# One DMA moved within SP's queue: a read back of turned attention weights, before or behind the next step's writes

## The chip, the cores and the metric

The kernel runs on one core of a Trainium2 chip. The metric is the device time of one execution in microseconds. Five engines take part: TensorE (PE) multiplies, VectorE (DVE), ScalarE (ACT) and GpSimd (POOL) do the work between, and SyncE (SP) issues the DMAs. Each engine runs its own instructions in the order in which the program lists them, and semaphores hold an instruction until what it needs is there.

## What is computed

A thresholded attention over 8 sequences, 8 heads, 576 tokens and head size 64, and behind it an expert layer with ELU.

```python
scores = scale * np.matmul(q, k.transpose(0, 1, 3, 2))
thresh = np.max(scores, axis=-1, keepdims=True) - tau
scores = np.where(scores >= thresh, scores, -1000000000.0)
attn = np.exp(scores - np.max(scores, axis=-1, keepdims=True))
attn = attn / (np.sum(attn, axis=-1, keepdims=True) + 1e-09)
attn_out = np.matmul(attn, v)
x = attn_out.transpose(0, 2, 1, 3).reshape(B * S, H * D)   # 4608 x 512
h = x @ w_in                                               # 512 x 2048
g = np.where(h > 0.0, h, np.exp(np.minimum(h, 0.0)) - 1.0)
out = g @ w_out                                            # 2048 x 512
```

All is in float32.

## The kernel before

**Pairs and steps.** The 64 heads are handled in 32 pairs of two heads. One step (a pair `pr` and a block `i`) takes 128 of the 576 query rows of both heads; blocks 0 to 3 are full, block 4 (`NC`) holds the last 64 rows of each head. Steps have numbers `n`. From number 20 on the five steps of a pair follow one another, so pair 7 is steps 35 to 39, and pair 8 is steps 40 to 44.

**One step.** TensorE makes the scores, VectorE the maxima, ScalarE the exponentials, VectorE and ScalarE mask them, and a normalization follows on POOL, VectorE or ScalarE (of step 41's two heads one is on ScalarE and one on POOL). Then the weights must be turned, so that TensorE can multiply them with the values. There are two ways. In one TensorE transposes 128x128 blocks. In the other (`turn_squares`, L859) VectorE transposes all 32x32 squares of the step into a tile `x` (L868, two buffers), SP writes it to a DRAM tile `there` in four DMAs of 144 KB, one for each quarter of the partitions (L893), and later `fetch` (L897) reads the step back in one DMA of 576 KB with the squares in their new places (L901; L910 for block 4). Blocks 0 and 1 of a pair are read into the tile `wTa`, blocks 2, 3 and 4 into `wTb`. Each of the two exists once. All steps around the change use the second way.

**Values.** `values(pr, 0)` (L915) multiplies `wTa` with the values of the pair, and so needs the reads of both block 0 and block 1: two matmuls at L925 and 16 at L930. A copy by ScalarE (L1060) puts the result into `xt`, the expert layer's input.

**Stages.** Steps 0 to 44 are the early stage. It shares TensorE with the plain expert layer of the first sequences (L1154). After step 44 the joined stage begins: the attention of the remaining pairs at L977, L1037, L1042 and L1050, and between them the expert layer of the earlier sequences, done with Strassen's seven products (L1678, L1818), whose sums of weights are read from DRAM as the tiles `sw` (L1250) and `t` (L1280). The end, from L2149 on, is the expert layer of the last two groups.

**What sets the order.** In the early stage every piece of work is a task with a due time, in the planner's own units. `task` (L1295) adds to a formula's due time an offset from the table `MOVED` under the task's name, such as `landed_40`. At the end (L1603) the tasks are issued in order of due time; `do` (L1299) first issues whatever a task names as needed. So a due time decides only the order in which instructions are listed, and with that the order on each engine and on SP's queue. Of a turned step, the task `turned` issues the transposes and the four writes, and the task `landed` issues the read back:

```python
if n < MIDDLE - 1:
    task(("turned", n), begin[n + 1] + 2.2, f"turn{k}", lambda pr=pr, i=i: turn_squares(pr, i), *norms)
if n < MIDDLE - 2:
    task(("landed", n), begin[n + 2] + 0.1, f"fetch{k}", lambda pr=pr, i=i: fetch(pr, i), ("turned", n), before)
```

Around the change the tasks that put a DMA on SP's queue come in this order (due times in brackets): `turned` 40 (1183), `landed` 39 (1188), `turned` 41 (1219), `landed` 40 (1222), `landed` 41 (1224), the output of pair 6, part 1 with a store to `xtail` (1225), `turned` 42 (1249), and then the loads of pair 9's values and of pair 10's keys. Between `turned` 41 and `landed` 40 stands an exponential of step 42 (1220), which is ScalarE's. `turned` 41 calls a normalization of step 41 on POOL that is needed and has not been issued by then. `values(8, 0)` comes much later in the list.

Of the kernel before, what the change touches and what calls it, by code (L numbers as in the profile page):

```python
# [131 lines left out]
    "landed_24": 486.39, "landed_25": 533.25, "landed_26": 984.59, "landed_27": 608.7, "landed_28": 593.43,  # L132
    "landed_29": 1100.39, "landed_3": 57.59, "landed_30": 602.25, "landed_31": 590.28, "landed_32": 704.7,
    "landed_33": 1197.19, "landed_34": 1068.39, "landed_35": 752, "landed_36": 789.43, "landed_37": 901.99,
    "landed_38": 847.93, "landed_39": 916.22, "landed_4": 23.49, "landed_40": 938.28, "landed_41": 938.99,
    "landed_42": 1089.42, "landed_5": 21.59, "landed_6": 85.49, "landed_7": 1161.59, "landed_8": 45.49, "landed_9":
    110.99, "late": 855.2, "load_k_1": 583, "load_k_10": 969.2, "load_k_2": 479, "load_k_3": 255, "load_k_4": 846,
    "load_k_5": 267.2, "load_k_6": 405.2, "load_k_7": 475.2, "load_k_8": 687.2, "load_k_9": 850.2, "load_q_1": 117,
# [2203 lines left out]
```

## Time and profile before

| What | us |
|---|---|
| median of 3 runs | 1265.59 |
| the runs, lowest and highest | 1262.77, 1266.57 |
| the profiled execution's own time | 1262.22 |
| its span, first to last instruction | 1260.4 |
| TensorE busy | 1245.6 |
| VectorE busy | 1041.4 |
| GpSimd busy | 729.4 |
| ScalarE busy | 636.4 |

The span is shorter than the time of the same execution, as it counts from the first instruction to the last. SP's DMA instructions are not counted as busy; the timeline of the queue gives for each how long SP took to issue it, and the DMA view how long from the issue until the data had landed. An idle time stands in brackets behind the group that it precedes, with what ended it as far as the trace can tell; "issue" there means that the trace shows no releaser.

Of the 16 DMA engines' time over the span, SP's queue takes 71.8%, in 323264 packets with 243.65 MB. The granted clock of TensorE was 0.999 on average.

### The profile page before, as it was taken

The page shows a single profiled execution, that of the slowest core. Times are in us where ns is not written, and L with a number is a line of the kernel's source. Part 1 is how long each engine was busy: PE and PEld are TensorE (multiplying, and loading weights), DVE is VectorE, ACT ScalarE, POOL GpSimd, SP SyncE. Part 2 cuts the span into 40 slices and gives each one's busy share as a digit, 9 for nine tenths or more (in the row PEclk, how much of TensorE's full clock was granted, in tenths as well). Part 3 has the DMA queues.
Part 4 walks back from the last instruction along what each step waited for, and adds up shares of the span by engine and source line. Part 5 has one row for each costly group of instructions (what it writes and reads, how often), then busy time and mean ns, then how long its engine had stood idle before and what let it go on. Part 6 is the DMA issues. An engine that isn't in the chain of part 4 may idle for free.

```text
span 1260.4 us, 21128 instructions
## 1 busy us (share of the span) xinstructions
PE 1245.6 (99%) x6598; PEld 956.5 (76%) x6598; DVE 1041.4 (83%) x2199; ACT 636.4 (50%) x1331; POOL 729.4 (58%) x1061
## 2 busy tenths in 40 slices
PE   8999999999999999999999999999999999999998
PEld 6675576467788787888788788878788887788876
DVE  7888777788898988898889889897889886776785
ACT  7999776664453526253534435352525352565321
POOL 4778655687575848676576757574867555122000
PEclk9999999999999999999999999999999999999999
DMA  7457788997989998898989888999889875000001
GB/s 144 146 172 181 173 243 229 264 279 196 233 238 254 247 252 228 228 264 221 268 211 259 221 243 218 255 247 251 234 229 264 221 224 173 20 1 1 1 34 34
DMA packets 325551, 245.74 MB, mean 195 GB/s; under 512 B 209216, under 2 KB 289984, under 8 KB 325440
## 3 DMA queue, kind: packets, MB, share of 16 engines
q1 hardware_dynamic: 323264, 243.65, 71.8%
q8 instruction: 52, 0.85, 0.3%
q10 hardware_dynamic: 2176, 0.75, 0.2%
q14 instruction: 59, 0.48, 0.1%
HBM read 154.53 MB, written 89.78 MB: 194 GB/s over the span
## 4 chain that ended last, share of the span: by engine, by line
PE 90%; DVE 4%; POOL 2%; DMA 2%; issue 1%; ACT 1%; SPq 1%; DVEq 0%; ACTq 0%; POOLq 0%
PE f L1678 22%; PE f L1818 22%; PE sc L977 8%; PE sc L1050 7%; PE f L2268 6%; PE f L2193 4%; PE f L1102 4%; PE sc L673 3%; PE f L1154 3%; PE pv L930 2%; PE f L2206 2%; PE rt L792 2%; PE sc L1042 1%; PE sc L1037 1%; DVE x L868 1%
## 5 line engine op out<-in xcount | busy, mean ns | idle before, releaser
L984 DVE TENSOR_REDUCE mx<-sc 128x1 f32<-128x576 f32 x207 | 148.3, 750 | 29.2 <-PE sc L977 25.2
L726 POOL TENSOR_SCALAR w<-w,rs 128x576 f32<-128x576 f32 x144 | 116.3, 816 | 70.3 <-DVE rs L789 70.1
L1004 ACT ACTIVATE w<-sc,mx 128x576 f32<-128x576 f32 x113 | 81.5, 740 | 115.0 <-DVE mx L984 98.0
L868 DVE STREAM_TRANSPOSE x<-w 128x512 f32<-128x512 f32 (+1 forms) x153 | 108.9, 744 | 13.1 <-POOL w L726 11.3
L996 POOL TENSOR_SCALAR th<-mx,ntau 128x2 f32<-128x2 f32 (+1 forms) x114 | 34.0, 298 | 132.8 <-DVE mx L984 132.8
L977 PE MATMUL sc<-kT,qT 64*128 64x448 f32 (+4 forms) x736 | 102.7, 416 | 0.0
L977 PEld LDWEIGHTS sc<-kT,qT 64*128 64x128 f32 x736 | 81.0, 186 | 24.3 <-issue 16.2
L1011 DVE SCALAR_TENSOR_TENSOR w<-sc,th,w 128x576 f32<-128x576 f32 x113 | 88.2, 810 | 9.5 <-ACT w L1004 9.2
L1678 PE MATMUL f<-xt,sw 128*128 128x256 f32 x384 | 93.6, 386 | 0.7 <-ACT g L1740 0.5
L1678 PE MATMUL f<-xt,w_in 128*128 128x256 f32 x384 | 92.0, 382 | 0.5 <-ACT w L1692 0.5
L1818 PE MATMUL f<-w_out,s 128*128 128x256 f32 x384 | 92.0, 382 | 0.1
L1818 PE MATMUL f<-w_out,g 128*128 128x256 f32 x384 | 92.0, 382 | 0.0
L1818 PE MATMUL f<-t,s 128*128 128x256 f32 x384 | 90.8, 379 | 0.0
L1678 PE MATMUL f<-x,w_in 128*128 128x256 f32 x384 | 90.8, 379 | 0.0
L726 POOL TENSOR_SCALAR e<-e,rs 128x576 f32<-128x576 f32 x91 | 67.4, 744 | 35.2 <-DVE rs L789 33.8
L1678 PEld LDWEIGHTS f<-xt,sw 128*128 128x128 f32 x384 | 69.3, 189 | 17.3 <-issue 5.0
L1678 PEld LDWEIGHTS f<-xt,w_in 128*128 128x128 f32 x384 | 71.9, 190 | 12.8 <-ACT w L1692 3.2
L1818 PEld LDWEIGHTS f<-w_out,g 128*128 128x128 f32 x384 | 72.0, 190 | 12.5 <-issue 3.2
L1818 PEld LDWEIGHTS f<-w_out,s 128*128 128x128 f32 x384 | 71.9, 190 | 12.5 <-issue 2.5
L1818 PEld LDWEIGHTS f<-t,s 128*128 128x128 f32 x384 | 72.8, 190 | 10.3 <-POOL s L1765 0.4
L1678 PEld LDWEIGHTS f<-x,w_in 128*128 128x128 f32 x384 | 72.9, 190 | 10.1 <-ACT s L1692 0.3
L1765 POOL TENSOR_TENSOR s<-g 128x256 f32<-128x256 f32 x96 | 75.0, 786 | 7.9 <-DVE g L1728 7.4
(345 smaller groups left out, 3113.5 us busy)
## 6 DMA issues: line engine op xcount, KB each, us to landing
there<-x SPq DMA_DIRECT2D x444, 144.0 KB, 3.5
wTb<-there SPq DMA_DIRECT2D x58, 576.0 KB, 6.4
wTa<-there SPq DMA_DIRECT2D x53, 576.0 KB, 5.0
sw<-win_sums SPq DMA_DIRECT2D x46, 384.0 KB, 4.7
t<-wout_sums SPq DMA_DIRECT2D x33, 512.0 KB, 6.1
qm<-in_q_dram SPq DMA_DIRECT2D x124, 72.0 KB, 4.9
wst<-in_moe_w_in_dram SPq DMA_DIRECT2D x16, 512.0 KB, 4.2
vm<-in_v_dram SPq DMA_DIRECT2D x64, 128.0 KB, 3.8
```

Source lines behind the costliest of these rows:

```text
L726: nc.gpsimd.tensor_scalar(wv, wv, st["rs"][:, h : h + 1], 1.0, ALU.mult, ALU.mult)
L868: nc.vector.transpose(x[:, :, c0 : c0 + nc_], src.rearrange("p (c g n) -> p g c n", c=nc_, n=T))
L977: on_banks(nc.tensor.matmul(o, qT[r, i * P : (i + 1) * P], kT[r, k0 : k0 + n], start=True, stop=True, skip_group_check=True), o)
L984: on_banks(nc.vector.tensor_reduce(st["mx"][:, h : h + 1], st["sc", h], axis=AX.XY if i == NC else AX.X, op=ALU.max, negate=True), st["sc" ...
L1004: on_banks(nc.scalar.activation(st["e", h], st["sc", h], AF.Exp, bias=st["mx"][:, h : h + 1]), st["sc", h])
L1011: on_banks(nc.vector.scalar_tensor_tensor(st["e", h], st["sc", h], st["th"][:, h : h + 1], st["e", h], ALU.is_ge, ALU.mult, accum_out=st[" ...
L1050: on_banks(nc.tensor.matmul(o, vm[:, h, c], parts[part][:, g0:g1, h * (NC + 1) + c], start=False, stop=(c == NC - 1), skip_group_check=Tru ...
L1102: nc.tensor.matmul(loc["ph"][:, k], w_in_at(j, ft * P, P), xts[g][:, j, hf * CT : (hf + 1) * CT], start=(j == 0), stop=(j == KJ - 1))
L1678: nc.tensor.matmul(loc["banks"][place], left[:, j], right[:, j], start=(begins and j == 0), stop=(j == 1), skip_group_check=True)
L1765: engine.tensor_tensor(o, x, y, op)
L1818: nc.tensor.matmul(place(m), lhs, rhs, start=(begins and v == 0), stop=(v == RU - 1), skip_group_check=True)
L2268: nc.tensor.matmul(banks8[2 * i + x // 2], h[:, tok], w, start=(f == 0 and x != 1), stop=(f == NFT - 1 and x != 0), skip_group_check=True)
```

## The change

One entry of the table `MOVED` is lowered by 3.6.

```diff
-    "landed_38": 847.93, "landed_39": 916.22, "landed_4": 23.49, "landed_40": 938.28, "landed_41": 938.99,
+    "landed_38": 847.93, "landed_39": 916.22, "landed_4": 23.49, "landed_40": 934.68, "landed_41": 938.99,
```

The due time of `landed` 40, the read back of pair 8's block 0 into `wTa`, goes from 1222.0 to 1218.4. It is now issued before `turned` 41 and not behind it. On SP's queue one DMA of 576 KB thus moves ahead of the four writes of step 41 (4 x 144 KB). No instruction is added, removed or altered, and no tile changes its size.

## The prediction

> **What bounds the kernel now.** I read the page first (busy time, chain), then the stretch of the change on TensorE, then the same stretch on SP's queue, then single transfers. Columns of the timelines: start us, us, queue or engine, line, operation, tiles, count.
>
> ```profile
> span 1260.4 us, 21128 instructions
> PE 1245.6 (99%) x6598; PEld 956.5 (76%) x6598; DVE 1041.4 (83%) x2199; ACT 636.4 (50%) x1331; POOL 729.4 (58%) x1061
> ...
> PE 90%; DVE 4%; POOL 2%; DMA 2%; issue 1%; ACT 1%; SPq 1%; DVEq 0%; ACTq 0%; POOLq 0%
> ```
>
> TensorE has work for 99% of the span and carries 90% of the chain. So 1260.4 - 1245.6 = 14.8 us is all that waits can give back, and only a wait of TensorE itself counts.
>
> ```profile
> 255.21 1.02 PE L1154 MATMUL f<-w_out,g 128*128 128x512 f32 x2
> 257.60 0.67 PE L925 MATMUL pv<-wTa,vd 128*128 128x256 f32 x2 [1.36 <-issue]
> 258.19 1.95 PE L930 MATMUL pv<-wTa,vm 128*64 128x256 f32 x16
> ```
>
> This is the value product of pair 8, part 0, the only reader of what the moved DMA brings. TensorE stands 1.36 us before it, its longest wait after the start of the kernel. The trace calls it "issue"; the queue shows what it is:
>
> ```profile
> 242.64 1.85 SPq L893 DMA_DIRECT2D there<-x  x4
> 244.61 0.57 SPq L910 DMA_DIRECT2D wTb<-there  x1
> 247.57 2.06 SPq L893 DMA_DIRECT2D there<-x  x4
> 249.79 0.34 SPq L901 DMA_DIRECT2D wTa<-there  x1
> 252.00 0.34 SPq L901 DMA_DIRECT2D wTa<-there  x1
> 252.38 0.43 SPq L1067 DMA_DIRECT2D xtail<-xs  x1
> 252.92 3.22 SPq L893 DMA_DIRECT2D there<-x  x4
> 257.52 0.60 SPq L560 DMA_DIRECT2D vd<-in_v_dram  x1
> ```
>
> In this order: W40, the four writes of step 40's turned weights (pair 8, block 0); R39, a read of pair 7; W41, the four writes of step 41 (pair 8, block 1); R40, the moved read; R41, the read of block 1. TensorE needs R40 and R41. Asked for one transfer at a time, the DMA view gives KB and us from issue to landing, here for R39, R40 and R41, and last the range over all transfers of the tile wTa:
>
> ```profile
> wTb<-there SPq DMA_DIRECT2D x1, 576.0 KB, 5.6
> ...
> wTa<-there SPq DMA_DIRECT2D x1, 576.0 KB, 4.9
> ...
> wTa<-there SPq DMA_DIRECT2D x1, 576.0 KB, 5.5
> ...
> DMA to landing us min/median/max: 3.9/5.0/8.0
> ```
>
> R39 lands at 244.61 + 5.6 = 250.2, R40 at 249.79 + 4.9 = 254.7, R41 at 252.00 + 5.5 = 257.5, a tenth before the product starts at 257.60. So R41, not the moved R40, ends the wait. The same view gives 2.8 us for W40's last write (issued 243.96, landed 246.8) and 3.0 for W41's last (issued 248.94, landed 251.9), and R41 is issued at 252.00, right after. Landings come in the order of issue: W40 246.8, R39 250.2, W41 251.9, R40 254.7, R41 257.5.
>
> **The change part by part.** Nothing is added or removed: the same DMA, with what it waits for, moves ahead of the four DMAs of W41 on SP's queue. By due times, R40 goes from 1222.0 to 1218.4 and passes W41 (1219) with the normalization it calls (POOL), and an exponential at 1220 (ACT). R40 is issued on SP alone, so POOL and ACT keep their orders, and no other DMA queue is passed.
>
> 1. **R40's own wait.** It must find W40 landed (246.8) and wTa free. Pair 7's product, the last reader of wTa, is over at 233.3 (16 matmuls from 231.32, 1.95 us). SP is free at 244.61 + 0.57 = 245.2, stands until 246.8 and issues by 246.8 + 0.34 = 247.2. Behind it stands W41, whose data VectorE finishes at 247.54 (two transposes from 246.11, 1.43 us); its first write went at 247.57. The new wait is hidden under that, with 0.4 us to spare; without the cover each microsecond delays W41 by one. Cost 0.
>
> 2. **R40's landing.** It now follows R39 (250.2) and not W41. A 576 KB read behind another lands 257.5 - 254.7 = 2.8 us after it (R41 behind R40, the nearest row, though smaller transfers ran beside it). By the rate of the stretch 250 to 260, 262 GB/s, 589,824 bytes take 2.25 us. I take 2.5: 252.7. R40 is two microseconds sooner, which nobody waits for.
>
> 3. **W41's landing.** In before its last write lands 251.9 - 250.2 = 1.7 us after R39. Behind R40 it lands at 252.7 + 1.7 = 254.4, which is 2.5 us later.
>
> 4. **R41.** It must wait for W41: issued at 254.5 and not 252.00. In before R40 was in flight in this gap; now nothing of size is. An empty queue is the case of the shortest landing of this tile, 3.9 us: 254.5 + 3.9 = 258.4, against 257.5, so **+0.9 us**. Bounds: 2.25 for R40 gives +0.65; 2.8 and the median landing of 5.0 give 254.8 + 5.0 = 259.8, +2.3. The first is nearer, as the median holds reads that queue behind others.
>
> [...]
>
> 5. **What stands behind R41 on SP.** The xtail store, the four writes of step 42, an output store and the loads of pairs 9 and 10 start up to 2.5 us later. The load at 257.52 stood in before until R41 had landed (SP was free at 256.72 + 0.46 = 257.18; the view of waits gives 0.3 us for wTa), so from there the lag is that of the landing, 0.9. Of what is read soonest, the 384 KB of sw issued at 271.10 land 4.2 us later, 275.3; their matmul starts at 277.95, so 2.6 us of lag are hidden. Cost 0.
>
> Behind the product TensorE goes on almost without a gap (10.00 us busy of 260 to 270), so 0.9 reaches the end. Sum: the profiled execution took 1262.22 us with a span of 1260.4; the span becomes 1261.3. The median shown, 1265.59, lies 3.4 above that execution; the same 0.9 on it gives **1266.5**.
>
> **The rivals.**
>
> *R41 lands sooner* (0.17). If W41's writes do not queue behind R40, as their sixteen engines may run apart, W41 lands at 251.9 as before, R41 is issued at 252.0 with R40 out of the way, and lands after 3.9 to 5.0, at 255.9 to 257.0: the gap shrinks by up to 1.36. Time 1265.59 - 1.36 = 1264.2. For it: TensorE has no other reason to stand there. Against it: the five landings in issue order. [...]
>
> *Slower, through SP's queue* (0.18). Place: the loads behind R41. If the lag of 2.5 to 2.8 is not given back at 257.52 and still exceeds 2.6 at the sw read of 271.10, it is paid on TensorE a second time: 1.2 (step 4 with R40 at 2.8) + 2.8 = +4.0, 1269.6. For it: SP issues nearly without a pause from 252 to 272, and step 42's writes (landing 259.2 in before) gate the buffer of VectorE's transposes at 261.27. Against it: the stand at 257.52.
>
> *The gap turns the clock down* (0.04). TensorE's gap would be 1.36 + 0.9 = 2.3 us, in the worst case 1.36 + 2.3 = 3.7. In this trace the granted clock stayed 1.00 over 250 to 260, and read 0.91 over 1250 to 1260, where matmuls stop at 1255.9. Were matmuls at half speed for as long as the worst gap, 3.7 us, half of it would be lost: 2.3 + 1.9 = +4.2, 1269.8. [...]
>
> *It does not do what it says* (0.06): some wait not seen here keeps R40 until W41 could have gone, and the landings change by less than 0.2. Time 1265.6.
>
> **How the numbers follow.** The forecast has 0.55, its own range +0.65 to +2.3. A measurement of this kernel can tell about 0.3% (3.8 us) from no change; its three runs alone lie 3.8 apart. The forecast and the first rival are inside that by mechanism; I leave 0.04 to scatter of either sign. Slower by over 0.3%: most of the second rival (0.14), half of the clock (0.02), scatter (0.04): 0.20. Faster: no wait of TensorE here is worth 3.8 us, so scatter (0.04) and a gain that I don't see (0.06): 0.10. Same: 0.70. Range: from the first rival's 1264.2 less 1.6 for scatter, 1262.6, to the second's 1269.6, cut at 1269.4.
>
> **What would show it.** Right: R40 issued near 247, landed near 252.7; W41 landed near 254.4; R41 issued after that; the gap before L925 near 2.3 us. Step 2 and 3 are wrong if W41 lands near 252; step 4 if R41 takes 5 us from an empty queue; step 5 if TensorE shows a new wait for sw between 270 and 290. The prediction is wrong if the gap is under 1.4 us, or the product starts on time and the end still moves.

## The result, and the profile after

| | before | after |
|---|---|---|
| median of 22 runs each, us | 1263.24 | 1266.55 |
| lowest and highest, us | 1262.38, 1267.13 | 1262.88, 1268.67 |
| profiled execution, us | 1262.22 | 1267.04 |
| its span, us | 1260.4 | 1265.3 |
| TensorE's gap ahead of L925, us | 1.36 | 2.90 |
| mean granted clock of the profiled execution | 0.999 | 0.997 |

The ratio of after to before is 1.0022, with a 95% interval of 1.0015 to 1.0028. The change made the kernel slower by a fifth of a per cent, some 2.8 us; the medians lie 3.3 apart. The median is where the prediction put it, but partly by luck: the three runs on which it was built had a median of 1265.59, and 22 runs of the same kernel have 1263.24. The base was 2.4 too high, and the effect, forecast as +0.9, was too small by about 2. The 0.3% that the prediction took as the least to be told from no change was more than needed: the interval is 0.13% wide.

First the page of after: the span and the engines' busy time.

```profile
span 1265.3 us, 21126 instructions
PE 1248.7 (99%) x6598; PEld 958.2 (76%) x6598; DVE 1041.2 (82%) x2199; ACT 635.7 (50%) x1331; POOL 727.6 (58%) x1061
```

The span grew by 4.9 us, in two parts. TensorE's idle time went from 14.8 to 1265.3 - 1248.7 = 16.6, so +1.8. Its busy time went from 1245.6 to 1248.7, so +3.1, with the same 6598 matmuls. A wait cannot do the second; the same work must have run slower. TensorE's timeline of after (start us, us, engine, line, tiles, count, and in brackets the idle time ahead) shows where:

```profile
255.44 1.02 PE L1154 MATMUL f<-w_out,g 128*128 128x512 f32 x2
259.37 1.22 PE L925 MATMUL pv<-wTa,vd 128*128 128x256 f32 x2 [2.90 <-DMA wTa<-there]
260.52 3.68 PE L930 MATMUL pv<-wTa,vm 128*64 128x256 f32 x16
```

The gap is 2.90, and the trace now names the transfer that ends it. Behind it the same 18 matmuls take 1.22 and 3.68 us, where before they took 0.67 and 1.95. The table of stretches tells why (stretch, us, then busy us and count of PE, PEld, DVE, ACT and POOL, the granted clock of TensorE, the DMA share, GB/s). Of after:

```profile
254.00:256.00 2.00, 2.00 (x10) 1.06 (x6) 1.86 (x6) 1.48 (x5) 1.55 (x2) 1.00 0.03 12
255.00:260.00 5.00, 2.10 (x7) 1.03 (x5) 4.73 (x7) 3.93 (x8) 4.86 (x7) 0.85 0.77 235
260.00:265.00 5.00, 5.00 (x22) 2.25 (x22) 0.81 (x2) 0.93 (x3) 3.50 (x4) 0.50 0.83 182
265.00:270.00 5.00, 5.00 (x26) 3.63 (x24) 2.27 (x6) 2.71 (x7) 2.21 (x3) 0.97 0.95 259
```

And two of the same stretches of before:

```profile
254.00:256.00 2.00, 2.00 (x8) 1.06 (x6) 1.87 (x6) 1.71 (x5) 1.55 (x3) 1.00 0.91 278
260.00:265.00 5.00, 5.00 (x28) 3.59 (x28) 2.99 (x7) 2.88 (x7) 4.73 (x6) 1.00 0.82 180
```

Two things are to be seen. The granted clock fell to 0.50 over 260 to 265, where it was 1.00; by the trace's record of it, the fall lasted from 258.52 to 265.34, 6.8 us. And over 254 to 256 the DMA engines stood almost empty: a share of 0.03 and 12 GB/s, where before they moved 278.

SP's queue in after, and then four single transfers in the order of issue (R39, R40, the last write of W41, R41; the last column is us from issue to landing):

```profile
244.80 0.82 SPq L910 DMA_DIRECT2D wTb<-there  x1
247.25 0.34 SPq L901 DMA_DIRECT2D wTa<-there  x1
247.80 2.31 SPq L893 DMA_DIRECT2D there<-x  x4
255.20 0.34 SPq L901 DMA_DIRECT2D wTa<-there  x1
...
259.37 0.78 SPq L560 DMA_DIRECT2D vd<-in_v_dram  x1
```

```profile
wTb<-there SPq DMA_DIRECT2D x1, 576.0 KB, 6.2
...
wTa<-there SPq DMA_DIRECT2D x1, 576.0 KB, 6.2
...
there<-x SPq DMA_DIRECT2D x1, 144.0 KB, 6.0
...
wTa<-there SPq DMA_DIRECT2D x1, 576.0 KB, 4.1
```

R39 lands at 251.0, R40 at 247.25 + 6.2 = 253.5, W41's last write (issued 249.09) at 255.1, R41 at 255.20 + 4.1 = 259.3, and the product starts at 259.37. From 250.11 to 255.20 SP only waits for W41, which stands behind R40. When W41 has landed nothing is left in flight, and R41 starts from empty engines: this is the stretch with 12 GB/s. L1154, the work ahead of the gap, starts 0.23 later than in before (255.44 against 255.21), a shift that this execution has from its start. The product is 259.37 - 257.60 = 1.8 later, of which 1.5 is thus the change.

From there the shift between the two traces grows from +1.8 at 259.4 to +4.6 when the clock is back (L1678 starts at 265.83 against 261.19). Near 563, where TensorE waits 0.17 us for a read of `sw`, another 0.3 is added. So lateness made about 1.5 us of it and the clock 2.9.

In the trace of after the record of the clock begins 5.93 us into the span and has full clock for 252.586 us, half for 6.827 and full for 1000.105; in that of before it begins at 5.41 and has full clock for 1252.691 us. These are 74, 2, 293 and 367 times 3.4133 us, a unit worked out from the four lengths. A window, here, is one such unit, counted from the changes in the trace's own record; the fall in after is two of them.

Over the 22 runs of after the mean granted clock takes several values. One window at half clock takes 3.41 x 0.5 / 1265 = 0.0013 off the mean, and the clock also falls at the end of the trace (to 0.50 from 1258.10 in before, 2.3 us ahead of the end of its span), which takes off 0.0009 in before and nothing in after. Ten runs have 0.997 or less (median 1267.45), as with two windows; five have 0.998 (1266.23), as with one. Seven have 0.999 or more (1264.71), which means none, or sometimes one: the profiled execution of experiment 9 has one window and reads 0.999. Of 35 runs of before that shared a chip with the first experiments, 27 have 0.999 or more (median 1263.05), six 0.998 and two 0.997 or less; no trace here shows where those eight lost their clock. So with little or no fall of the clock the change costs about 1264.71 - 1263.05 = 1.7, and the two windows at half clock cost about 1267.45 - 1264.71 = 2.7 more.

### The profile page after: what moved, and what is told of

Its sections match the earlier page's. It is cut to its first block, busy times and chain, and to the rows that moved or that the text cites. A ratio compares the mean times of both kernels' runs of the same rounds, so it can differ in the third digit from the quotient of the medians.

```text
span 1265.3 us, 21126 instructions
## 1 busy us (share of the span) xinstructions
PE 1248.7 (99%) x6598; PEld 958.2 (76%) x6598; DVE 1041.2 (82%) x2199; ACT 635.7 (50%) x1331; POOL 727.6 (58%) x1061
## 3 DMA queue, kind: packets, MB, share of 16 engines
q1 hardware_dynamic: 323264, 243.65, 71.7%
## 4 chain that ended last, share of the span: by engine, by line
PE 88%; DVE 4%; DMA 3%; ACT 1%; POOL 1%; issue 1%; SPq 1%; DVEq 0%; ACTq 0%; POOLq 0%
PE f L1818 23%; PE f L1678 21%; PE sc L977 7%; PE sc L1050 7%; PE f L2268 6%; PE f L2193 4%; PE f L1102 4%; PE sc L673 3%; PE f L1154 3%; PE pv L930 2%; PE f L2206 2%; PE rt L792 2%; PE sc L1042 1%; PE sc L1037 1%; DMA there<-x 1%
## 5 line engine op out<-in xcount | busy, mean ns | idle before, releaser
L1678 PE MATMUL f<-xt,sw 128*128 128x256 f32 x384 | 93.7, 386 | 0.8 <-ACT g L1740 0.5
L1678 PE MATMUL f<-xt,w_in 128*128 128x256 f32 x384 | 91.9, 382 | 0.5 <-ACT w L1692 0.5
L1678 PE MATMUL f<-x,w_in 128*128 128x256 f32 x384 | 90.8, 379 | 0.0
L1678 PEld LDWEIGHTS f<-xt,sw 128*128 128x128 f32 x384 | 69.3, 189 | 17.7 <-issue 5.5
L1678 PEld LDWEIGHTS f<-xt,w_in 128*128 128x128 f32 x384 | 72.0, 190 | 12.6 <-ACT w L1692 2.9
L1678 PEld LDWEIGHTS f<-x,w_in 128*128 128x128 f32 x384 | 72.9, 190 | 10.1 <-ACT s L1692 0.3
```

Of the source, the lines that this page charges most:

```text
L1678: nc.tensor.matmul(loc["banks"][place], left[:, j], right[:, j], start=(begins and j == 0), stop=(j == 1), skip_group_check=True)
```

## The experiments

The theory after the result: R41 waits for W41, which queues behind R40; that makes the product 1.5 to 1.7 us late; and the longer gap lets TensorE's clock fall, in some executions, for 2.7 more. The rivals: that the lateness alone makes the whole difference, that the clock falls for another reason than the gap, and that the transfers are ordered only within an issuing engine's queue. In this section "low clock" counts runs with a mean granted clock of 0.997 or less. Each kernel is set against runs of before on the same chip; the experiments used three chips, with 35, 33 and 23 runs of before.

### 1. After, with twelve idle transposes in the gap (a_fill12)

They give TensorE something to do ahead of the product, into a PSUM tile that the product then overwrites.

```diff
+        if (pr, part) == (8, 0):
+            for _ in range(12):
+                transpose(pv[:, :P], idents[-1])
```

> The changed kernel, with 12 idle transposes on TensorE right ahead of the value product of pair 8, part 0 (their result is overwritten); SP's queue is that of the changed kernel. Theory (R41 lands later, and the longer gap of TensorE then turns its clock down): R41 still lands 1.6 to 1.9 us later than in before, but the gap before L925 shrinks from 2.9 to about 1 us, the granted clock stays 1.00 over 255 to 270, the 18 matmuls behind the gap take 2.5 us as in before and not 4.8, and the time is 1.5 to 2 us above before (ratio 1.0012 to 1.0016). Rival (the matmuls behind the gap are slow since the DMAs beside them are later, or the lag of SP's queue is paid further on; the clock only goes along): the 18 matmuls still take near 4.8 us, or another wait opens, and the ratio stays at 1.002 or more.

Measured: 1264.96 against 1263.17, ratio 1.0012 [1.0003, 1.0021], low clock in 1 of 12 runs. TensorE's timeline, and below it one stretch:

```profile
256.86 1.47 PE L792 MATMUL pv<-s 128*128 128x128 f32 x12
259.40 0.70 PE L928 MATMUL pv<-wTa,vd 128*128 128x256 f32 x2 [1.07 <-DMA wTa<-there]
260.03 1.95 PE L933 MATMUL pv<-wTa,vm 128*64 128x256 f32 x16
```

```profile
260.00:265.00 5.00, 5.00 (x34) 3.31 (x34) 3.17 (x8) 2.12 (x6) 4.10 (x4) 1.00 0.80 181
```

The product starts at 259.40, as late as in after, though 0.8 of that stands in this execution from its start (0.2 in after). The idle time just ahead is 1.07, the clock stays at 1.00 and the matmuls take 0.70 and 1.95 again. What is left, 1.8 us by the medians, is lateness. The lateness alone does not make the whole difference, and with the gap mostly filled low clock came in 1 of 12 runs, where after has 10 of 22. Twelve runs are few; experiment 6 puts the same question the other way round.

### 2. Before, with five such transposes (b_fill5)

The same edit on the kernel before, with `range(5)`: does the smaller gap of before cost clock too?

> The kernel before, with 5 idle transposes ahead of the same product: its gap of 1.36 us shrinks to about 0.5. Theory (the clock falls only where TensorE stands long enough): in before the gap of 1.36 never or seldom does it, so median and spread stay, ratio 0.999 to 1.0005. Rival (the few long runs of before, 1265.6 to 1267.1, come from this gap as well): the long runs go, the highest run is under 1264.5, ratio below 0.9995.

Measured: 1263.31 against 1263.17, ratio 1.0000 [0.9992, 1.0008], low clock in 0 of 12. The fill costs nothing and brings nothing; since before had low clock in only 2 of 35, twelve runs cannot tell whether the fill removes it.

### 3. After, with R40 in two halves around W41 (split_r40)

The first half of R40 stays ahead of W41's writes, the second goes behind them, ahead of R41.

```diff
+    second_half = []
+
     def fetch(pr, i):
+        while second_half:
+            second_half.pop()()
...
-        if i < NC:
+        if (pr, i) == (8, 0):
+            to = wT[:, g0 : g0 + NT].rearrange("p g c n -> p g (c n)")
+            nc.sync.dma_start(to[:, :2], back[:, :2])
+            second_half.append(lambda: nc.sync.dma_start(to[:, 2:], back[:, 2:]))
+        elif i < NC:
```

> The changed kernel with R40 cut in two reads of 288 KB, the first where R40 is (ahead of W41), the second behind W41, ahead of R41. Theory (transfers land strictly in the order of issue, each byte ahead of W41 delays it): W41's last write lands 1.2 us sooner than in the changed kernel, near 253.8, R41 lands near 257.7, the gap is about 1.6 us, the clock stays up in most runs, ratio 1.0002 to 1.0008. Rival (what counts is that SP's queue waits for W40 ahead of W41, or that a read stands ahead of the writes at all): R41 lands near 259.3 as in the changed kernel, ratio 1.0015 or more.

Measured: 1262.93 against 1263.17, ratio 0.9995 [0.9987, 1.0004], low clock in 0 of 12. SP's queue and TensorE's timeline:

```profile
246.53 0.34 SPq L906 DMA_DIRECT2D wTa<-there  x1
247.86 2.63 SPq L893 DMA_DIRECT2D there<-x  x4
250.59 0.39 SPq L907 DMA_DIRECT2D wTa<-there  x1
253.82 0.34 SPq L909 DMA_DIRECT2D wTa<-there  x1
```

```profile
257.91 0.67 PE L933 MATMUL pv<-wTa,vd 128*128 128x256 f32 x2 [1.26 <-issue]
```

W41 now has half as much in front of it and lands at 253.68; R41 goes at 253.82 and not at 255.20, and the gap is 1.26. It is the bytes of R40 ahead of W41 that cost the time, not the order of the instructions. Half of them still delay W41, which landed at 251.9 in before. But R41 then takes 4.0 us and not the 5.5 of before, so it lands at 257.8, only 0.3 later, and 0.3 of shift stands in this execution from its start. By the time nothing is lost, where 1.0002 to 1.0008 was expected.

### 4. Before, with R39 ahead of W40 (r39_early)

The same kind of move one step earlier in the queue, by the same table.

```diff
-    "landed_38": 847.93, "landed_39": 916.22, "landed_4": 23.49, "landed_40": 938.28, "landed_41": 938.99,
+    "landed_38": 847.93, "landed_39": 910.22, "landed_4": 23.49, "landed_40": 938.28, "landed_41": 938.99,
```

> The kernel before, with the read R39 (pair 7, block 4) issued ahead of the four writes W40 and not behind them. Theory (the transfers are one queue, so the work ahead of R41 ends sooner if the pause in which the DMA engines stand at R39's start is filled): R39 lands near 247.3, W41 near 250.8, R41 is issued near 251 and lands near 255.6, TensorE's gap of 1.36 closes, 1.0 to 1.4 us faster than before, ratio 0.9989 to 0.9993. Rival (W40 is then later by as much, and W41 and R41 with it): R41 lands at 257 to 258, ratio 0.9996 to 1.0005.

Measured: 1263.29 against 1263.17, ratio 1.0001 [0.9992, 1.0011], low clock in 1 of 12. My expectation of the landings fell; the time is the rival's, though R41 landed at 259.5, later than either had it. The profiled execution, SP's queue, the transfer of R39, TensorE and two stretches, each one window of the clock:

```profile
242.49 0.57 SPq L910 DMA_DIRECT2D wTb<-there  x1
```

```profile
wTb<-there SPq DMA_DIRECT2D x1, 576.0 KB, 6.9
```

```profile
259.55 0.67 PE L925 MATMUL pv<-wTa,vd 128*128 128x256 f32 x2 [3.13 <-issue]
260.15 1.95 PE L930 MATMUL pv<-wTa,vm 128*64 128x256 f32 x16
```

```profile
254.97:258.38 3.41, 1.45 (x5) 0.52 (x3) 3.35 (x7) 2.41 (x5) 3.27 (x6) 1.00 0.88 260
258.38:261.80 3.42, 2.25 (x18) 1.36 (x18) 2.24 (x4) 1.69 (x4) 3.42 (x4) 1.00 0.75 216
```

R39 took 6.9 us and landed at 249.35, two microseconds later than I had put it; R41, issued at 253.34, took 6.1. The gap in this execution was 3.13, longer than in after, and yet the clock stayed at 1.00 and the matmuls ran at full speed. The length of the gap alone does not decide. The border between two windows, at 258.38, cuts this gap: 1.96 us of it lie in the first (3.41 less 1.45) and 1.17 in the second.

### 5. After, with five transposes (a_fill5)

A smaller fill, to see how the share of low clock goes with the gap.

> The changed kernel with 5 idle transposes on TensorE ahead of the value product, not 12: the gap before L925 is about 2.1 us, between the 1.07 of the run with 12 and the 2.90 of the changed kernel. Theory (the clock falls with a chance that grows with the length of the gap): a mean clock of 0.997 or less shows in fewer runs than in the changed kernel (10 of 22) and in more than with 12 transposes (1 of 12), ratio 1.0012 to 1.0020. Rival (any gap over about 1.4 us does it, or none under 2.9): as many low clocks as in the changed kernel and 1.0022, or none and 1.0012.

Measured: 1264.87 against 1263.72, ratio 1.0013 [1.0002, 1.0024]; gap 2.21; low clock in 3 of 11, with the highest run at 1268.67. The counts lie between those of after and of twelve transposes, as expected, but 11 runs are too few to tell 3 from either.

### 6. Before, with four more writes behind W41 (b_extra_w)

Another cause of the same gap: step 41's squares are written a second time, to a DRAM tile that nothing reads. The order of R40 is that of before.

```diff
+        if (pr, i) == (8, 1):
+            again = dram.tile([NT, T, NT, NCH * T], FP32, name="again", bufs=1)
+            for p in range(NT):
+                nc.sync.dma_start(
+                    again[:, :, p].rearrange("c k n -> k c n"), x[p * T : (p + 1) * T].rearrange("k c j n -> k c (j n)")
+                )
```

> The kernel before, order unchanged, with four more writes of 144 KB behind W41 and ahead of R40 (step 41's tile once more, into a DRAM tile that nobody reads). Theory (bytes queued ahead of R41 make it late, and the gap makes the clock fall, wherever R40 stands): W41 lands as in before, R40 and R41 land 1.8 to 2.3 us later than in before, the gap is 3.2 to 3.6 us, most runs show a mean clock of 0.997 or less, ratio 1.0022 to 1.0032. Rival (the loss of the change is tied to R40's place ahead of W41, in SP's wait for W40): R41 is at most 1 us later, ratio under 1.001.

Measured: 1266.78 against 1263.72, ratio 1.0018 [1.0009, 1.0027], low clock in 7 of 11. TensorE and one stretch:

```profile
260.58 1.19 PE L931 MATMUL pv<-wTa,vd 128*128 128x256 f32 x2 [3.98 <-DMA there<-x]
261.70 3.68 PE L936 MATMUL pv<-wTa,vm 128*64 128x256 f32 x16
```

```profile
260.00:265.00 5.00, 4.42 (x18) 2.22 (x18) 1.83 (x3) 0.44 (x3) 3.64 (x4) 0.50 0.62 138
```

With R40 where it was before, the gap made in another way gives the same picture: the clock at 0.50, and 1.19 and 3.68 us for the same matmuls. On this chip before has low clock in 3 of 33 runs. The fall comes with the gap, not with the moved DMA as such. In size the expectation missed: R41 landed 2.5 us later than in before (260.4 against 257.5, less 0.4 of shift) and not 1.8 to 2.3, the gap is longer than the 3.2 to 3.6 expected, and the ratio lies below the 1.0022 to 1.0032.

### 7. After, with R40 issued by ScalarE (a_act)

ScalarE's DMAs have a queue of their own: in before q1 carries 243.65 MB for SP, and q10 the 0.75 MB of ScalarE's eight. If order held only within a queue, W41 would be free of R40.

```diff
-            nc.sync.dma_start(wT[:, g0 : g0 + NT].rearrange("p g c n -> p g (c n)"), back)
+            queue = nc.scalar if (pr, i) == (8, 0) else nc.sync
+            queue.dma_start(wT[:, g0 : g0 + NT].rearrange("p g c n -> p g (c n)"), back)
```

> The changed kernel with R40 issued by ScalarE and not by SP, at the same place of the program. Theory (the order of landing is that of one queue; two queues share the DMA engines): W41 no longer lands behind R40, at 252.5 to 253.5 instead of 255.1, R41 is issued right behind it and lands near 257, the gap is 0.7 to 1.6 us, ratio 0.9993 to 1.0008; ScalarE stands about 0.6 us for W40. Rival (the 16 DMA engines serve in the order of issue whatever queue a DMA is on): W41 lands near 254.5 to 255, R41 near 259, ratio 1.0015 or more.

Measured: 1264.70 against 1263.72, ratio 1.0010 [1.0001, 1.0018], low clock in 1 of 11. The gap, 2.28, is shorter than in after because the work ahead of it starts 0.7 later (256.18 against 255.44). The timeline of the two queues, and single transfers: R40 and the first write of W41.

```profile
247.37 0.36 ACTq L902 DMA_DIRECT2D wTa<-there  x1
247.70 1.88 SPq L893 DMA_DIRECT2D there<-x  x4
255.70 0.34 SPq L902 DMA_DIRECT2D wTa<-there  x1
```

```profile
wTa<-there ACTq DMA_DIRECT2D x1, 576.0 KB, 6.0
...
there<-x SPq DMA_DIRECT2D x1, 144.0 KB, 5.9
```

R40 lands at 253.3 and the first write of W41 at 253.6, the last at 255.5: still in the order of issue, though on two queues, and R41 goes no sooner (255.70). The expectation that the queue of the issuer decides fell, and its rival was right on the landings, though the time is under the 1.0015 that it gave. The DMA view over 251.0 to 252.5 gives for each queue its packets, MB and share of the engines' time; q1 is SP's queue, which then carries W41 alone, and q10 is ScalarE's, with R40:

```profile
q1 hardware_dynamic: 362, 0.38, 71.0%
q10 hardware_dynamic: 47, 0.18, 29.7%
```

The two queues moved data side by side: 0.38 MB of W41 and 0.18 MB of R40 in the same 1.5 us. Still the first write, a quarter as large as R40, did not land ahead of it: 5.9 us for 144 KB beside 6.0 for 576 KB. So the two transfers shared the engines (71.0 and 29.7% of their time) and the landings kept the order of issue; what held back the landing of the first write, this run does not show.

### 8. After, with R40 and R41 in halves (split_both)

Experiment 3, and R41 as two DMAs.

```diff
...
+        elif (pr, i) == (8, 1):
+            to = wT[:, g0 : g0 + NT].rearrange("p g c n -> p g (c n)")
+            for r in (slice(0, 2), slice(2, 4)):
+                nc.sync.dma_start(to[:, r], back[:, r])
...
```

> The kernel with R40 cut in two halves around W41, and R41 cut in two halves as well, so that R41's first half needs only the first two writes of W41. Theory (the loss left there is the time from W41's last landing to R41's first data): R41's first half is issued 0.8 us sooner than R41 in the kernel with R40 alone cut, all of R41 lands near 257.0 to 257.3, the gap is 0.6 to 0.9 us, ratio 0.9988 to 0.9996. Rival (each read pays a slow start of its own, so two halves cost more than one): R41 lands at 257.8 or later, ratio 0.9995 to 1.0005.

Measured: 1262.58 against 1263.72, ratio 0.9992 [0.9983, 1.0001], low clock in 0 of 11; gap 1.19. The gap is longer than the 0.6 to 0.9 expected, but the profiled execution was the slowest of the eleven (1266.19), late by 0.7 us from its start and by 1.5 at the work ahead of the gap, so its landings say little. The interval still holds 1.

### 9. After, with R41 in quarters (a_quarters)

Each quarter of R41 reads what one of W41's four writes brought, so it can go as soon as that write has landed.

```diff
-        if i < NC:
+        if (pr, i) == (8, 1):
+            to = wT[:, g0 : g0 + NT].rearrange("p g c n -> p g (c n)")
+            for p in range(NT):
+                nc.sync.dma_start(to[:, p], back[:, p])
+        elif i < NC:
```

> The changed kernel, R40 whole and ahead of W41, with R41 cut in four reads of 144 KB, each of which needs one write of W41 alone. Theory (the lateness of R41 is the stretch of some 2 us in which the DMA engines stand empty between W41's last landing and R41's first data): the first quarter is issued 1.1 us sooner than R41 in the changed kernel, the engines no longer stand empty, all of R41 lands 0.8 to 1.3 us sooner, the gap is 1.6 to 2.1 us and not 2.9, ratio 1.0002 to 1.0012. Rival (R41 is late by its place behind 576 KB more, not by the empty stretch): it lands at most 0.3 us sooner, ratio 1.0015 or more.

Measured: 1264.49 against 1263.12, ratio 1.0009 [1.0000, 1.0017], low clock in 2 of 12. TensorE, and two stretches:

```profile
258.39 0.67 PE L929 MATMUL pv<-wTa,vd 128*128 128x256 f32 x2 [1.86 <-DMA wTa<-there]
259.00 3.63 PE L934 MATMUL pv<-wTa,vm 128*64 128x256 f32 x16
```

```profile
254.00:256.00 2.00, 2.00 (x10) 1.06 (x6) 1.86 (x6) 1.40 (x5) 1.54 (x2) 1.00 0.47 131
255.61:259.03 3.42, 1.56 (x7) 0.43 (x5) 3.26 (x7) 2.43 (x4) 3.28 (x6) 1.00 0.88 259
```

The first quarter goes at 254.04 and the last lands at 258.26. The engines are half full over 254 to 256 (0.47, where after has 0.03), and the gap shrinks to 1.86. So the empty queue between W41 and R41 was a part of the lateness. This execution shows something else too: the clock fell, at 259.03 and for 3.41 us, after a gap of only 1.86. All of this gap lies in one window, the second stretch above (3.42 less 1.56).

### 10. After, with R40 in halves and R41 in quarters (split_quarters)

Experiments 3 and 9 together.

> R40 cut in halves around W41 and R41 cut in four. Theory (as in the kernel with both cut in halves, with the first piece of R41 another 0.4 us sooner): the gap is 0.4 to 1.0 us, no run shows a mean clock under 0.998, ratio 0.9985 to 0.9994. Rival (each read pays its own issue and start): no better than with R41 whole, 0.9995 or more.

Measured: 1261.80 (1261.41 to 1263.71) against 1263.12, ratio 0.9987 [0.9978, 0.9995], low clock in 0 of 11. SP's queue, TensorE and one stretch:

```profile
247.63 1.87 SPq L893 DMA_DIRECT2D there<-x  x4
249.60 0.62 SPq L907 DMA_DIRECT2D wTa<-there  x1
251.02 2.37 SPq L911 DMA_DIRECT2D wTa<-there  x4
```

```profile
255.28 1.02 PE L1166 MATMUL f<-w_out,g 128*128 128x512 f32 x2
256.13 0.60 PE L937 MATMUL pv<-wTa,vd 128*128 128x256 f32 x2
258.84 1.19 PE L1049 MATMUL sc<-kT,qT 64*64 64x288 f32 x8 [0.23 <-ACT w L753]
```

```profile
254.00:256.00 2.00, 2.00 (x9) 1.21 (x7) 1.86 (x6) 1.64 (x5) 1.54 (x3) 1.00 0.90 245
```

The first quarter of R41 goes at 251.02 while W41's other writes are still on their way (the last lands at 252.9), the engines stay full (0.90), and the product at 256.13 follows L1154 with no gap. Of the 1.36 us of before, 0.23 come back at 258.84 as a new wait for ScalarE, and 0.30 a little later. This kernel is faster than before, by 0.05 to 0.22%.

All kernels beside one another, by the gap of the profiled execution. The third column is TensorE's idle time in the emptiest window around the gap, worked out as above; the fourth says whether the clock fell in that execution.

| kernel | gap, us | idle in one window, us | clock fell | low clock in |
|---|---|---|---|---|
| b_extra_w | 3.98 | 2.53 | yes | 7 of 11 |
| r39_early | 3.13 | 1.96 | no | 1 of 12 |
| after | 2.90 | 2.06 | yes | 10 of 22 |
| a_act | 2.28 | 1.33 | no | 1 of 11 |
| a_fill5 | 2.21 | 1.52 | no | 3 of 11 |
| a_quarters | 1.86 | 1.86 | yes | 2 of 12 |
| before | 1.36 | 1.36 | no | 5 of 91 |
| split_r40, split_both | 1.26, 1.19 | 1.26, 1.19 | no | 0 of 23 |
| a_fill12 | 1.07 | 1.07 | no | 1 of 12 |
| b_fill5 | 0.79 | 0.79 | no | 0 of 12 |
| split_quarters | none | 0.53 | no | 0 of 11 |

The window orders the falls far better than the gap does: the clock fell at 1.86, 2.06 and 2.53 us and stayed up at 1.52 and less, with r39_early's 1.96 the one exception. The gap of one execution stands for the kernel only roughly: r39_early's profiled execution landed R41 after 6.1 us, and a median like that of before suggests that most of its runs had a shorter gap.

## Why the prediction was right or wrong

**What bounds the kernel: right.** TensorE bounds it, and the reader of R41 is where the change is felt. That the trace's "issue" was R41's landing is borne out: in after the same gap is named as a wait for that DMA.

**Step 1, R40's own wait: right.** It was issued at 247.25, and W41's first write went at 247.80, 0.23 later than in before, which is the shift that this execution has from its start.

**Step 2, R40 lands 2.5 behind R39: right in size.** 253.5 - 251.0 = 2.5. R39 itself landed later than the 250.2 on which the step was built; 0.23 of that is the execution's shift, and 0.55 is a slower R39 (6.2 for 5.6), which the forecast had as given.

**Step 3, W41 1.7 behind R40: right.** 255.07 - 253.47 = 1.6. That W41 is bound to R40 by its bytes is shown by experiment 3: with half of R40 ahead of it, it landed at 253.68.

**Step 4, R41 from empty engines: right in kind, too small.** R41 took 4.1 for the 3.9 that I took, and was issued at 255.20 for 254.5. The product came 1.5 us late and not 0.9, inside the bounds of 0.65 and 2.3. The runs with little or no fall of the clock say the same: 1.7. Of this 0.6, 0.2 is R41's own landing and most of the rest R39. The traces show 4.1 in after and 4.0 in experiment 3, both from nearly empty engines.

**Step 5, SP's lag costs 0: right where it looked.** The load that stands behind R41 went at 259.37, 1.85 later than in before, as late as the landing. TensorE shows no new wait for sw between 270 and 290, and so the second rival, the price through SP's queue, did not happen. One new wait for sw, of 0.17 us, stands at 563.67; whether the lag made it isn't shown.

**What failed: the sum ended at step 4.** I wrote that 0.9 reaches the end because TensorE goes on without a gap, and gave "the gap turns the clock down" a chance of 0.04. By the mean clock it happened in 10 of 22 runs with two windows, and in at least 5 more with one. The 0.04 was my estimate, from the one profile that I had, in which the clock read 1.00 behind a gap of 1.36; nothing in it showed that a gap of 2.3 would leave the clock up. Experiments 1 and 6 show that the gap makes the fall (fill it, and low clock is down to 1 of 12 runs; make it in another way, and it comes in 7 of 11), experiments 4 and 9 that the length of the gap alone does not sort the falls (3.13 without a fall, 1.86 with one); the idle time in one window does, but for one trace (a fall at 1.86, 2.06 and 2.53, none at 1.52 and less, and none at r39_early's 1.96). The price that I worked out for it, +1.9, was too small too. Half speed is what the traces show (a clock of 0.50, with 1.22 and 3.68 us for the 0.67 and 1.95 of before), but I let it last for as long as the gap; the fall lasted 3.41 or 6.83 us, and costs 1264.71 to 1267.45, 2.7 us, in the runs with two windows. With ten of 22 runs at that price, 10/22 x 2.7 = 1.2, and 1.5 of lateness, the sum would have been +2.7, close to the 2.8 that the ratio gives.

**The rival "R41 lands sooner": wrong.** W41 landed behind R40, even when R40 came from another engine's queue (experiment 7). **"It does not do what it says": wrong.** R40 landed at 253.5 for 254.7, and W41 at 255.1 for 251.9.

**What stays open.** Why R39 took 6.2 us in after and 6.9 in experiment 4 isn't settled. In which executions the clock falls at a given gap is settled only in part: the idle time in one window fits eleven of the twelve traces, but each kernel has one trace, no run set the windows' phase, and 1.96 without a fall beside 1.86 with one keeps the bound open. Before too reads 0.998 in 22 of its 91 runs, and split_quarters, which has no gap, in 1 of 11, so some windows are probably lost elsewhere; no trace shows where.

## What to carry to other kernels

Ahead of a write that a later read must wait for, count the bytes in the queue and not the instructions: a read of 576 KB put in front moved the write's landing by 3 us (255.1 against 251.9, less 0.2 of shift), and half of it by 1.5 (253.7, less 0.3), which the next read, 1.5 us shorter, made up. Read back in pieces that each depend on one write; here the pieces kept the engines full while the last write was under way (a DMA share of 0.90 over 254 to 256 in experiment 10, where after has 0.03), and that is where this kernel gained (0.9987 [0.9978, 0.9995]). Price a gap of TensorE like these not only by its length but also by a chance of a low clock behind it (here it fell with gaps of 1.86, 2.90 and 3.98 us, and low clock came in 2 of 12, 10 of 22 and 7 of 11 runs), and look at the clock of many runs, as one profile shows a single draw: r39_early's had a gap of 3.13 and a clock of 1.00.

## What the runs showed of the hardware

**The clock fell for one window of 3.41 us or for two, behind a window with 1.86 us or more of idle time.** The granted clock went to 0.50 for 3.41 us (experiment 9) or 6.83 us (after, experiment 6), and began at 258.52 (after) and 259.13 (experiment 6), in the last half of the gap, and at 259.03 (experiment 9), 0.6 us behind its end. The gaps were 1.86 (experiment 9), 2.90 (after) and 3.98 us (experiment 6) long. Each of these falls began at the border behind a window in which TensorE had stood for 1.86 to 2.53 us. In after and experiment 6 the gap reached 0.85 and 1.45 us into the next window, and the clock stayed low for a second one; in experiment 9 nothing of the gap was left, and one window was all. Here is the window of after, ahead of the fall:

```profile
255.10:258.52 3.42, 1.36 (x5) 0.43 (x3) 3.29 (x6) 2.41 (x5) 3.28 (x6) 1.00 0.65 187
```

The length of the gap did not decide it: the clock fell with a gap of 1.86 us and stayed up behind one of 3.13, where the fuller of the two windows had 1.96 us of idle time. The kernels with gaps under 1.4 us had low clock in 6 of 149 runs.

**The DMAs landed in the order of issue, across queues too.** In before and in after all 1284 landed so, eight of them ScalarE's, and in experiment 7 a write of SP's queue issued 0.33 us after a read of ScalarE's landed 0.3 us behind it, though it was a quarter as large and its queue's packets ran beside the read's.

**The read that waited for the write found the engines empty.** The stretches of after in halves of a microsecond, with the columns as before:

```profile
254.50:255.00 0.50, 0.50 (x3) 0.40 (x4) 0.43 (x5) 0.49 (x3) 0.06 (x1) 1.00 0.01 2
255.50:256.00 0.50, 0.50 (x3) 0.14 (x1) 0.43 (x2) 0.50 (x2) 0.50 (x1) 1.00 0.00 0
256.00:256.50 0.50, 0.47 (x2) 0.00 (x0) 0.46 (x2) 0.50 (x1) 0.44 (x3) 1.00 0.92 129
```

W41's packets are over at 254.56, its last landing is known at 255.07, R41 is issued at 255.20, and its packets begin at 256.18. So 0.5 us passed from the last packets to the landing and 1.0 from the issue to the first packets. With a single read in line both were empty time (a DMA share of 0.03 over 254 to 256); with four reads and four writes, and half of R40 between them, it was filled (0.90, experiment 10).
